# One rotation of three PSUM banks for all transposes and small products, and a changed order of the opening, in a cluster attention followed by two feed-forward layers

## The chip, the cores and the metric

The kernel runs on one core of a Trainium2 chip. The metric is the device time of one execution in microseconds (us), the median of several runs. Engines are named as in the profile: PE is TensorE (PEld its weight loads), DVE is VectorE, ACT is ScalarE, POOL is GpSimd, SP is SyncE, which issues the DMAs here.

## What is computed

```python
q_assign = np.argmax(np.einsum('bhsd,hcd->bhsc', q_n, c_n), axis=-1)
k_assign = np.argmax(np.einsum('bhsd,hcd->bhsc', k_n, c_n), axis=-1)
mask = q_assign[:, :, :, None] == k_assign[:, :, None, :]
scores = np.where(mask, scale * np.matmul(q, k.transpose(0, 1, 3, 2)), -1000000000.0)
attn = np.exp(scores - np.max(scores, axis=-1, keepdims=True))
attn = attn / (np.sum(attn, axis=-1, keepdims=True) + 1e-09)
x = np.matmul(attn, v)                          # 2 x 8 heads, 768 x 64, 16 clusters a head
h = x @ w_in;  x = (np.maximum(h, 0) + alpha * np.minimum(h, 0)) @ w_out      # 1536 x 512 x 2048
h = x @ w2_in; x = (np.maximum(h, 0) + np.log1p(np.exp(-np.abs(h)))) @ w2_out
```

Queries, keys and centroids are normalized first (`q_n`, `k_n`, `c_n`). All of it is float32; the kernel splits each operand into a high part that TensorE takes at full rate and a low rest, and adds three products.

## The kernel before

**Attention** works on 8 pairs of heads. A pair has 12 units, numbered from 0 (so pair 1 starts at unit 12): 2 heads, 3 groups of 256 queries, 2 tiles of 128 queries. The loop over units `u` puts out, in this order: on PE the scores of unit `u` (tile `s`, L721 and L722, four matmuls into a pool of two buffers); on ACT the exponential of unit `u-1` (tile `e`, L736); on DVE the negated row maximum of unit `u` (`nm`, L727); then the steps set down for an early place in `u`; then on PE the six transposes of `e` of unit `u-2`, three to a PSUM bank (`pt`, L749), which ACT copies out as a high part (`ph`, L765) and DVE as the rest (`pl`, L769); then on PE six products with the values (`o`, L779); then the steps set down for a late place in `u`.

**The preparation of a pair** is cut into named steps. For pair `n` they are: `sq`, `fold`, `inv` (squares of the token tile `tok`, their sums on POOL, inverse norms `rinv` through ACT, DVE and POOL, L133 to L142); `hik`, `hiq`, `lok`, `lq` (high and low parts of the transposed tile `dim`, `lq` on DVE, L510); `dk`, `dq` (products with the cluster centroids, tile `dps`, L525, three matmuls each for keys and queries, 0 and 1 for the two halves of the sequence); `de` (ACT copies `dps` to `dsb`, L533); `dt` (six small transposes of `dsb`, L550); `dn`, `mx`, `eq`, `m2` (the arg max, on DVE and POOL, L564 to L604); `ot` (three transposes of the one-hot rows, L614); `mr` (ACT makes mask rows `mrow`, L622); `mk` (SP copies these by DMA into the operands `mq` and `mk` of the scores, L671, L672); `va` (values split on POOL, L686, L687). After a pair, `finish` spreads the sums by three transposes to a bank (`rp_`, L863) and DVE divides (L872).

**What sets the order.** All engines run in the order in which the program puts out instructions (`tc.manual_schedule`). The tables STEADY, FIRST, SECOND, THIRD and LAST give each step a unit, counted from 24 units ahead of its pair: `dk0=4` is the late place of unit 4 of the pair two ahead, `de0=5.5` the early place of unit 6. Pair 1 uses SECOND, pair 2 THIRD, pairs 3 to 6 STEADY. What comes ahead of unit 0 stands in the list PRELUDE (name and pair). `warm` puts out transposes of the identity whose results nobody reads (L334).

**PSUM** has eight banks: `ps_t` two (the `pt` tiles, and a few of pair 0), `ps_o` one, `ps_m` one (all small tiles: `dps`, `dt`, `ot`, `rp_`, and the fourth output chunk of the feed-forward layers), `ps_s` two of two banks each for the scores. A new tile waits until the last reader of the tile that had its bank is done.

**The feed-forward layers** follow: matmuls of 128 x 512 into four banks (`ps_h`, which take over the banks of the scores), and output products in four chunks `c` (accumulators `acc`, L287 and L1310): chunks 0 and 1 in `ps_t`, 2 in `ps_o`, 3 in `ps_m`. Their weights come as 64-bit words and are converted on ACT, DVE and POOL beside the matmuls.

Of the kernel before, what the change touches and what calls it, by code (L numbers as in the profile page):

```python
# [24 lines left out]
    sq0=0, hik0=1, hik1=2, lok=2, hiq0=3, hiq1=3, sq1=3, lt=3.5, fold0=4, lq0=4, dk0=4, dq0=5, de0=5.5,  # L25
    lq1=6.5, dk1=6, dq1=7, de1=7.5, fold1=8, fold2=9, dt=10, ld=10, inv0=11, inv1=11.5, inv2=12, dn=12.5,
# [7 lines left out]
    dl0=12, dl1=12, inv0=12, de0=12.5, de1=12.5, inv1=12.5, inv2=13, dt=13, dn=13.5, op0a=13.5, mx=14,  # L34
    op0b=14.5, op0c=15.5, eq=16, op1a=17.5, m2=18, op1b=18, op1c=18.5, ot0=20, mr0=20.5, ot1=21, mr1=21.5,
    mk0=21.5, va0=22, mk1=22.5, va1=24, lv=25, go=23,
)
THIRD = dict(STEADY, hik0=3, sq0=3, hik1=3, hiq0=4, lok=4, hiq1=5, sq1=5, lt=5.5, lq0=5, dk0=5, fold0=7)
# [22 lines left out]
def kernel(  # L61
# [139 lines left out]
    ps_t = ctx.enter_context(tc.tile_pool(name="ps_t", bufs=2, space=PSUM, reuse_waits="tile"))  # L201
    ps_o = ctx.enter_context(tc.tile_pool(name="ps_o", bufs=1, space=PSUM, reuse_waits="tile"))
    ps_m = ctx.enter_context(tc.tile_pool(name="ps_m", bufs=1, space=PSUM, reuse_waits="tile"))
# [70 lines left out]
    def second(k):  # L274
        layer, g, f = mlp_steps[k]
        gh, gl = acts.pop(k)
        h_, l_ = weights[layer, f][2:4]
        opens, closes = (layer, f) in starts, (layer, f) in ends
        if opens:
            for c in range(4):  # L280
                pool, tag = ((ps_t, "t"), (ps_t, "t"), (ps_o, "o"), (ps_m, "m"))[c]
                accs[c] = pool.tile([P, 512], F32, tag=tag, name=f"acc{c}")
        for c in range(4):
            cs = slice(c * P, (c + 1) * P)
            prods = ((h_[:, cs], gh), (h_[:, cs], gl), (l_[:, cs], gh))
            for n, (a_, b_) in enumerate(prods):
                nc.tensor.matmul(  # L287
                    accs[c], lhsT=a_, rhs=b_, start=opens and n == 0, stop=closes and n == 2
                )
# [28 lines left out]
    with ExitStack() as actx:  # L318
# [40 lines left out]
        def load_tok(n):  # L359
            if n < len(pairs):  # L360
                if n == 1:
                    toks[n] = ap2.tile([P, J, 2, P], F32, tag="ph", name="tok", bufs=2)
                else:
                    toks[n] = ap1.tile([P, J, 2, P], F32, tag="tok", name="tok")
                nc.sync.dma_start(out=toks[n], in_=qk_tok[pairs[n]])
# [26 lines left out]
        cps = ps_m.tile([P, 512], F32, tag="m", name="cps")  # L392
# [35 lines left out]
        def steps_of(n):  # L428
# [87 lines left out]
            def dots(t, prods):  # L516
                if prods[0] == (1, 0):
                    if early and t == 0:
                        q["dps", t] = ps_o.tile([P, 512], F32, tag="o", name="dps")
                    else:  # L520
                        q["dps", t] = ps_m.tile([P, 512], F32, tag="m", name="dps")
# [22 lines left out]
            def _():  # L544
                if first_:
                    dt = ps_t.tile([P, 512], F32, tag="t", name="dt")
                else:
                    dt = ps_m.tile([P, 512], F32, tag="m", name="dt")
# [59 lines left out]
            def onehot(t):  # L608
                if first_:
                    q["ot", t] = ps_t.tile([P, 512], F32R, tag="t", name="ot")  # L610
                else:
                    q["ot", t] = ps_m.tile([P, 512], F32R, tag="m", name="ot")
# [207 lines left out]
        def finish(n):  # L820
# [34 lines left out]
            for t in range(2):  # L855

                def spread(t):
                    if last and t == 1:
                        rp_ = ps_t.tile([P, 512], F32, tag="t", name="rp_")
                    else:  # L860
                        rp_ = ps_m.tile([P, 512], F32, tag="m", name="rp_")
# [66 lines left out]
        at(1)(lambda: warm(8))  # L928
# [363 lines left out]
    def out_product(q, g, c, tick):  # L1292
# [4 lines left out]
        def run():  # L1297
            pool, tag = ((ps_t, "t"), (ps_t, "t"), (ps_o, "o"), (ps_m, "m"))[c]
# [44 lines left out]
    def last_product():  # L1343
# [4 lines left out]
        for n, (pool, tag) in enumerate(((ps_m, "m"), (ps_t, "t"))):  # L1348
# [289 lines left out]
```

## Time and profile before

| | |
|---|---|
| Median of 3 runs | 781.36 us (781.09 to 781.46) |
| The profiled execution | 782.5 us, its span 780.7 us |
| PE, DVE, ACT, POOL busy | 760.1, 650.6, 552.2, 507.9 us |
| Mean granted clock of PE | 0.996 |

The span runs from the first to the last instruction; the execution's own time is 1.8 us longer. Busy time of PE counts a matmul from its start to its modelled end, and matmuls overlap, so it says little by itself: where PE is close to its limit, the distance from one start to the next tells more. The attention ends near 266 us; the rest is the two layers.

### The profile page before, as it was taken

To read this page: it belongs to the slowest core of one execution; us is meant where nothing else is said; L and a number is where in the kernel's file an instruction comes from. 1 tells how busy PE (TensorE), PEld (TensorE's weight loads), DVE (VectorE), ACT (ScalarE), POOL (GpSimd) and SP (SyncE) were. 2 spreads that over 40 slices of the span, in tenths; PEclk is the share of its full clock that TensorE was granted. 3 is DMA by queue.
4 is the path that set the end of the run, shared out by engine and by line. 5 is a ranking of instruction groups with operands and counts; after the bars stand their busy time and mean duration, and the time that the engine had idled before them with its cause. 6 is when DMAs were issued, how large, how long until landed. Compare 5 with 4: busy or idle time off the path is not lost.

```text
span 780.7 us, 12017 instructions
## 1 busy us (share of the span) xinstructions
PE 760.1 (97%) x4073; PEld 651.5 (83%) x4073; DVE 650.6 (83%) x1015; ACT 552.2 (71%) x1130; POOL 507.9 (65%) x510
## 2 busy tenths in 40 slices
PE   7699999999999899999999999999999999999998
PEld 6598999999999788788888888887888888888887
DVE  6778889889899767489967768799989898998965
ACT  5788999999899878365766766856965555655530
POOL 5666677886643545478758778598785766756810
PEclk9999999999999999999999999999999999999999
DMA  9857467566452350012112121211220302212004
GB/s 248 217 147 194 126 179 183 143 158 163 101 132 81 106 182 34 0 55 82 37 72 81 55 81 60 76 54 33 103 80 29 108 27 81 82 54 82 1 0 162
DMA packets 27101, 75.92 MB, mean 97 GB/s; under 512 B 4480, under 2 KB 7680, under 8 KB 27040
## 3 DMA queue, kind: packets, MB, share of 16 engines
q1 hardware_dynamic: 27040, 75.16, 32.9%
q8 instruction: 32, 0.52, 0.3%
q14 instruction: 29, 0.24, 0.1%
HBM read 49.36 MB, written 3.15 MB: 67 GB/s over the span
## 4 chain that ended last, share of the span: by engine, by line
PE 81%; ACT 6%; POOL 4%; DVE 3%; issue 3%; DMA 2%; SPq 0%; POOLq 0%; ACTq 0%; DVEq 0%
PE acc L1310 26%; PE hp L1146 9%; PE x L1146 8%; PE pt L749 7%; PE o L779 7%; PE v L1146 4%; PE acc L287 4%; PE s L721 4%; PE s L722 4%; PE hp L235 3%; PE z L1146 2%; DMA tok<-in_qk_tok_dram 1%; PE dps L525 1%; POOL sq L470 1%; ACT e L736 1%
## 5 line engine op out<-in xcount | busy, mean ns | idle before, releaser
L727 DVE TENSOR_REDUCE nm<-s 128x1 f32<-128x768 f32 x96 | 91.1, 949 | 17.4 <-PE s L722 17.2
L769 DVE TENSOR_TENSOR pl<-pt,ph 128x384 fp32r<-128x384 f32 x192 | 97.6, 550 | 8.3 <-ACT ph L765 7.6
L765 ACT CAST ph<-pt 128x384 fp32r<-128x384 f32 x192 | 84.1, 488 | 15.4 <-PE pt L749 14.7
L736 ACT ACTIVATE e<-s,nm 128x768 f32<-128x768 f32 x96 | 88.2, 918 | 3.4 <-DVE nm L727 2.9
L749 PE MATMUL pt<-ident,e 128*128 128x128 f32 x576 | 83.6, 278 | 6.0 <-DVE pl L769 6.0
L749 PEld LDWEIGHTS pt<-ident,e 128*128 128x128 f32 x576 | 67.4, 142 | 18.5 <-DVE pl L769 15.0
L1326 DVE TENSOR_TENSOR y<-y,acc 128x512 f32<-128x512 f32 x97 | 65.9, 680 | 15.9 <-PE acc L1310 15.6
L1333 POOL TENSOR_TENSOR y<-y,n 128x512 f32<-128x512 f32 x42 | 57.0, 1362 | 32.2 <-ACT n L1323 32.2
L1310 PE MATMUL acc<-oh,gl 128*128 128x512 f32 x190 | 74.0, 389 | 0.0
L1310 PE MATMUL acc<-oh,gh 128*128 128x512 f32 x190 | 74.0, 389 | 0.0
L1310 PE MATMUL acc<-ol,gh 128*128 128x512 f32 x190 | 74.0, 389 | 0.0
L175 DVE SCALAR_TENSOR_TENSOR r<-raw,r 128x512 uint32<-128x512 uint32 x64 | 65.6, 1025 | 4.0 <-issue 3.1
L721 PE MATMUL s<-ak,aq 128*128 128x384 f32 x192 | 68.9, 359 | 0.0
L722 PE MATMUL s<-mk,mq 80*128 80x384 f32 x192 | 65.7, 342 | 2.5 <-DVE mk L633 2.5
L182 POOL TENSOR_TENSOR tw<-m,r 128x512 uint32<-128x512 uint32 x26 | 34.0, 1308 | 48.4 <-DVE r L175 47.4
L187 POOL TENSOR_TENSOR il<-tw,ih 128x512 fp32r<-128x512 f32 x26 | 34.3, 1320 | 34.0 <-ACT ih L186 34.0
L182 POOL TENSOR_TENSOR t<-m,r 128x512 uint32<-128x512 uint32 x38 | 50.1, 1318 | 9.1 <-DVE r L175 9.1
L187 POOL TENSOR_TENSOR ol<-t,oh 128x512 fp32r<-128x512 f32 x32 | 46.8, 1461 | 11.6 <-ACT oh L186 11.6
L170 DVE TENSOR_SCALAR m<-m 128x512 f32<-128x512 f32 x64 | 47.5, 742 | 3.9 <-ACT m L166 3.8
L1146 PE MATMUL hp<-xl,ih 128*128 128x512 f32 x120 | 46.9, 391 | 1.4 <-DVE xl L1365 1.4
L1310 PE MATMUL acc<-gl,oh 128*128 128x512 f32 x120 | 46.8, 390 | 0.0
L1146 PE MATMUL hp<-xh,il 128*128 128x512 f32 x120 | 46.7, 390 | 0.0
(295 smaller groups left out, 2357.7 us busy)
## 6 DMA issues: line engine op xcount, KB each, us to landing
raw<-in_w_in_dram SPq DMA_DIRECT2D x32, 512.0 KB, 3.2
raw<-in_w_out_dram SPq DMA_DIRECT2D x32, 512.0 KB, 3.3
tok<-in_qk_tok_dram SPq DMA_DIRECT2D x8, 768.0 KB, 6.0
ak<-hi SPq DMA_DIRECT2D x31, 192.0 KB, 3.0
dim<-in_qk_dim_dram SPq DMA_DIRECT2D x6, 768.0 KB, 5.7
aq<-hi SPq DMA_DIRECT2D x16, 192.0 KB, 3.6
aq<-lo SPq DMA_DIRECT2D x16, 192.0 KB, 4.0
rawv<-in_v_dram SPq DMA_DIRECT2D x8, 384.0 KB, 4.0
```

What stands on the lines that cost most here:

```text
L182: nc.gpsimd.tensor_tensor(out=t.bitcast(U32), in0=mu, in1=r, op=ALU.add)
L187: nc.gpsimd.tensor_tensor(out=low, in0=t, in1=high.bitcast(F32), op=ALU.subtract)
L721: nc.tensor.matmul(s[:, c, 0:HS], lhsT=aq[:, qs], rhs=ak[:, ks], start=True, stop=False)
L722: nc.tensor.matmul(s[:, c, 0:HS], lhsT=mq[:, qs], rhs=mk[:, ks], start=False, stop=True)
L727: nc.vector.tensor_reduce(out=nm, in_=st[u]["s"][:, :, 0:HS], axis=AX.XY, op=ALU.max, negate=True)
L736: nc.scalar.activation(out=e.rearrange("p (a j) c -> p a (j c)", a=2), in_=st[u]["s"][:, :, 0:HS], func=AF.Exp, bias=st[u]["nm"], scale=1. ...
L749: nc.tensor.transpose(pt[:, j * P : (j + 1) * P], st[u]["e"][:, 3 * a + j, :], ident)
L765: nc.scalar.copy(out=dh, in_=src)
L769: nc.vector.tensor_tensor(out=dl, in0=src, in1=dh.bitcast(F32), op=ALU.subtract)
L1146: nc.tensor.matmul(o, lhsT=x_, rhs=y_, start=start and j == 0 and n == 0, stop=stop and j == len(ah) - 1 and n == 2, skip_group_check=chain,)
L1310: nc.tensor.matmul(acc, lhsT=a_, rhs=b_, start=s_ == 0 and n == 0, stop=s_ == 1 and n == 2)
L1326: nc.vector.tensor_tensor(out=y, in0=y, in1=acc, op=ALU.add)
```

## The change

All tiles of `ps_m` go into `ps_t`, which gets three banks; the pool `ps_m` is gone. Steps get other places: in STEADY `dk0` goes from unit 4 to 5 (where `dq0` is), `lq1` from the early place of unit 7 to the late place of unit 6, `dk1` from 6 to 7 (where `dq1` is), `dt` from 10 to 12. In THIRD (pair 2) `dk0` and `dq0` go to 6, `lq1` and `de0` to 7, `dk1` and `dq1` to 8. In SECOND (pair 1) `inv2` and `dt` go half a unit later, `eq` one unit earlier, `va1` half a unit later. In PRELUDE `lq0 1` and `lq1 1` go behind the mask rows of pair 0. The token tile of pair 0 is loaded by two DMAs, and the eight `warm` transposes of unit 1 are left out.

```diff
-    sq0=0, hik0=1, hik1=2, lok=2, hiq0=3, hiq1=3, sq1=3, lt=3.5, fold0=4, lq0=4, dk0=4, dq0=5, de0=5.5,
-    lq1=6.5, dk1=6, dq1=7, de1=7.5, fold1=8, fold2=9, dt=10, ld=10, inv0=11, inv1=11.5, inv2=12, dn=12.5,
+    sq0=0, hik0=1, hik1=2, lok=2, hiq0=3, hiq1=3, sq1=3, lt=3.5, fold0=4, lq0=4, dk0=5, dq0=5, de0=5.5,
+    lq1=6, dk1=7, dq1=7, de1=7.5, fold1=8, fold2=9, dt=12, ld=10, inv0=11, inv1=11.5, inv2=12, dn=12.5,
...
 SECOND = dict(
-    dl0=12, dl1=12, inv0=12, de0=12.5, de1=12.5, inv1=12.5, inv2=13, dt=13, dn=13.5, op0a=13.5, mx=14,
-    op0b=14.5, op0c=15.5, eq=16, op1a=17.5, m2=18, op1b=18, op1c=18.5, ot0=20, mr0=20.5, ot1=21, mr1=21.5,
-    mk0=21.5, va0=22, mk1=22.5, va1=24, lv=25, go=23,
+    dl0=12, dl1=12, inv0=12, de0=12.5, de1=12.5, inv1=12.5, inv2=13.5, dt=13.5, dn=13.5, op0a=13.5, mx=14,
+    op0b=14.5, op0c=15.5, eq=15, op1a=17.5, m2=18, op1b=18, op1c=18.5, ot0=20, mr0=20.5, ot1=21, mr1=21.5,
+    mk0=21.5, va0=22, mk1=22.5, va1=24.5, lv=25.5, go=23,
 )
-THIRD = dict(STEADY, hik0=3, sq0=3, hik1=3, hiq0=4, lok=4, hiq1=5, sq1=5, lt=5.5, lq0=5, dk0=5, fold0=7)
+THIRD = dict(STEADY, hik0=3, sq0=3, hik1=3, hiq0=4, lok=4, hiq1=5, sq1=5, lt=5.5, lq0=5, dk0=6, dq0=6, de0=6.5, lq1=7, dk1=8, dq1=8, de1=8.5, fold0=7)
...
-    "dh1 1", "op1a 0", "op1b 0", "op1c 0", "minus_alpha", "dn 0", "mx 0", "eq 0", "m2 0", "lq0 1",
-    "lq1 1", "ot0 0", "ot1 0", "rq0 0", "rk1 0", "rk0 0", "rq1 0", "go 0", "mr0 0", "mr1 0", "mk1 0", "ld 1",
+    "dh1 1", "op1a 0", "op1b 0", "op1c 0", "minus_alpha", "dn 0", "mx 0", "eq 0", "m2 0",
+    "ot0 0", "ot1 0", "rq0 0", "rk1 0", "rk0 0", "rq1 0", "lq0 1", "lq1 1", "go 0", "mr0 0", "mr1 0", "mk1 0", "ld 1",
...
-    ps_t = ctx.enter_context(tc.tile_pool(name="ps_t", bufs=2, space=PSUM, reuse_waits="tile"))
+    ps_t = ctx.enter_context(tc.tile_pool(name="ps_t", bufs=3, space=PSUM, reuse_waits="tile"))
     ps_o = ctx.enter_context(tc.tile_pool(name="ps_o", bufs=1, space=PSUM, reuse_waits="tile"))
-    ps_m = ctx.enter_context(tc.tile_pool(name="ps_m", bufs=1, space=PSUM, reuse_waits="tile"))
...
-                pool, tag = ((ps_t, "t"), (ps_t, "t"), (ps_o, "o"), (ps_m, "m"))[c]
+                pool, tag = ((ps_t, "t"), (ps_t, "t"), (ps_o, "o"), (ps_t, "t"))[c]
...
-                nc.sync.dma_start(out=toks[n], in_=qk_tok[pairs[n]])
+                for cut in (slice(0, 3), slice(3, J)) if n == 0 else (slice(0, J),):
+                    nc.sync.dma_start(out=toks[n][:, cut], in_=qk_tok[pairs[n]][:, cut])
...
-                        q["dps", t] = ps_m.tile([P, 512], F32, tag="m", name="dps")
+                        q["dps", t] = ps_t.tile([P, 512], F32, tag="t", name="dps")
...
-                    q["ot", t] = ps_m.tile([P, 512], F32R, tag="m", name="ot")
+                    q["ot", t] = ps_t.tile([P, 512], F32R, tag="t", name="ot")
...
-        at(1)(lambda: warm(8))
```

The other lines of the diff put `cps`, `dt`, `rp_` and the accumulators of chunk 3 from `ps_m` into `ps_t` in the same way.

**PE in the opening**, units 1 and 2 (`s` scores, `wps` the warm transposes, `pt` transposes of the probabilities of unit 0, `dt` small transposes of pair 1). Before:

```order
L550 MATMUL dt<-ident,dsb 128x64 x6
L334 MATMUL wps<-ident 128x128 x8
L721 MATMUL s<-ak,aq 128x384
L722 MATMUL s<-mk,mq 128x384
L721 MATMUL s<-ak,aq 128x384
L722 MATMUL s<-mk,mq 128x384
L749 MATMUL pt<-ident,e 128x128 x6
```

With the change:

```order
L721 MATMUL s<-ak,aq 128x384
L722 MATMUL s<-mk,mq 128x384
L721 MATMUL s<-ak,aq 128x384
L722 MATMUL s<-mk,mq 128x384
L550 MATMUL dt<-ident,dsb 128x64 x6
L749 MATMUL pt<-ident,e 128x128 x6
```

The scores of unit 2 stand ahead of the small transposes, which are followed by the transposes of the probabilities at once.

**POOL at the end of pair 0**, unit 12 (`s_810` and `s_792` the norms of pair 2 in work, `vv` values of pair 1, `sq` squares of pair 3). Before:

```order
L139 TENSOR_TENSOR s_810<-s_810,s_793 128x24
L686 CAST vv<-rawv 128x6x64
L687 TENSOR_TENSOR vv<-rawv,vv 128x6x64
L141 TENSOR_SCALAR s_810<-s_810 128x24
L453 TENSOR_TENSOR sq<-tok 128x768
```

With the change:

```order
L139 TENSOR_TENSOR s_792<-s_792,s_775 128x24
L141 TENSOR_SCALAR s_792<-s_792 128x24
L453 TENSOR_TENSOR sq<-tok 128x768
L686 CAST vv<-rawv 128x6x64
L687 TENSOR_TENSOR vv<-rawv,vv 128x6x64
```

The two instructions of the values have gone behind the norms.

**PE at a pair's end**, from unit 9 of pair 2 on. Before:

```order
L614 MATMUL ot<-identr,oh 64x128 x3
L721 MATMUL s<-ak,aq 128x384
L722 MATMUL s<-mk,mq 128x384
L721 MATMUL s<-ak,aq 128x384
L722 MATMUL s<-mk,mq 128x384
L749 MATMUL pt<-ident,e 128x128 x6
L779 MATMUL o<-ph,vv 128x256 x6
L550 MATMUL dt<-ident,dsb 128x64 x6
```

With the change, two units later (unit 0 of pair 3):

```order
L721 MATMUL s<-ak,aq 128x384
L722 MATMUL s<-mk,mq 128x384
L749 MATMUL pt<-ident,e 128x128 x6
L779 MATMUL o<-ph,vv 128x256 x6
L550 MATMUL dt<-ident,dsb 128x64 x6
L721 MATMUL s<-ak,aq 128x384
```

The small transposes `dt` have left unit 10 and stand between units 0 and 1 of the next pair.

## Rows read from the trace of the kernel before

**Rows 1.** Windows by stage: us; busy PE, PEld, DVE, ACT, POOL; clock; DMA share.

```profile
0.00:22.80 22.80, 16.54 (x95) 14.73 (x95) 15.31 (x30) 13.75 (x28) 13.64 (x45) 0.93 0.89 236
22.80:53.20 30.40, 25.85 (x189) 22.76 (x189) 24.29 (x38) 23.65 (x56) 18.91 (x24) 1.00 0.76 189
53.20:85.40 32.20, 30.63 (x219) 28.46 (x218) 26.74 (x47) 27.18 (x66) 22.08 (x29) 0.95 0.59 153
85.40:231.70 146.30, 146.29 (x1095) 136.14 (x1093) 133.86 (x239) 137.20 (x335) 103.19 (x131) 1.00 0.62 152
231.70:266.60 34.90, 31.45 (x231) 28.30 (x230) 31.30 (x59) 33.20 (x78) 13.63 (x16) 1.00 0.31 103
266.60:780.70 514.10, 509.32 (x2257) 421.09 (x2256) 419.11 (x607) 317.19 (x572) 336.42 (x267) 1.00 0.19 66
```

**Rows 2.** Chain of waits in the opening: start us, us, what.

```profile
4.08 11.19 DMA tok<-in_qk_tok_dram
...
22.19 0.34 ACT s L133
...
22.78 0.97 ACT e L736 x2
...
25.12 1.02 PE wps L334 x8
```

**Rows 3.** Timeline of ACT, then PE, in the opening; idle before in brackets.

```profile
8.71 1.58 ACT L451 ACTIVATE sq<-tok 128x768 f32<-128x768 f32 x2 [2.15 <-DMA tok<-in_qk_tok_dram]
...
20.97 0.41 PE L722 MATMUL s<-mk,mq 80*128 80x384 f32 x1 [2.52 <-DVE mk L633]
...
37.85 0.39 PE L525 MATMUL dps<-lo,chz 128*64 128x384 f32 x1 [1.94 <-DMA rest<-tmp]
...
53.16 0.34 PE L721 MATMUL s<-ak,aq 128*128 128x384 f32 x1
...
59.83 1.01 PE L749 MATMUL pt<-ident,e 128*128 128x128 f32 x6 [1.57 <-DVE pl L769]
```

**Rows 4.** Timeline of DVE, then POOL, then DVE in the opening.

```profile
33.41 2.12 DVE L587 SCALAR_TENSOR_TENSOR dn<-dn,rank 128x384 f32<-128x384 f32 x1
...
56.40 1.01 POOL L687 TENSOR_TENSOR vv<-rawv,vv 128x384 fp32r<-128x384 f32 x1
57.49 0.21 POOL L141 TENSOR_SCALAR s<-s 128x24 f32<-128x24 f32 x1
...
57.74 0.30 DVE L142 RECIPROCAL rinv<-s 128x24 f32<-128x24 f32 x1 [1.50 <-POOL s L141]
```

**Rows 5.** Chain of waits in pair 3, from its unit 0 to the next pair.

```profile
115.97 0.66 PE pt L749 x6
...
117.33 0.33 PE s L721
...
118.19 1.00 PE pt L749 x6
...
120.61 0.99 PE pt L749 x6
...
142.19 0.52 PE dt L550 x6
...
145.16 0.18 PE s L722
```

**Rows 6.** SP's issue of the mask rows of pair 4, and its landing time.

```profile
142.41 0.58 SPq L672 DMA_DIRECT2D mk<-mrow  x1
...
mk<-mrow SPq DMA_DIRECT2D x1, 48.0 KB, 2.1
```

**Rows 7.** Windows: the granted clock (third number from the end) around two falls.

```profile
13.10:16.50 3.40, 3.40 (x18) 3.29 (x17) 3.12 (x7) 3.24 (x7) 1.82 (x1) 0.50 1.02 213
16.50:24.00 7.50, 4.11 (x26) 3.12 (x24) 6.08 (x7) 4.70 (x10) 6.49 (x9) 1.00 0.81 165
...
60.90:64.30 3.40, 3.40 (x17) 3.30 (x15) 2.55 (x4) 2.09 (x5) 3.24 (x4) 0.50 0.82 178
```

More of the change, by code (lines that the diff above doesn't have):

```diff
@@ L391 @@
         warm(18, ps_s)
-        cps = ps_m.tile([P, 512], F32, tag="m", name="cps")
+        cps = ps_t.tile([P, 512], F32, tag="t", name="cps")
         nc.tensor.transpose(cps[:, 0:P], cnrm, ident)
@@ L547, in _ @@
                 else:
-                    dt = ps_m.tile([P, 512], F32, tag="m", name="dt")
+                    dt = ps_t.tile([P, 512], F32, tag="t", name="dt")
                 for j in range(J):
@@ L860, in spread @@
                     else:
-                        rp_ = ps_m.tile([P, 512], F32, tag="m", name="rp_")
+                        rp_ = ps_t.tile([P, 512], F32, tag="t", name="rp_")
                     for j in range(3):
@@ L1297, in run @@
         def run():
-            pool, tag = ((ps_t, "t"), (ps_t, "t"), (ps_o, "o"), (ps_m, "m"))[c]
+            pool, tag = ((ps_t, "t"), (ps_t, "t"), (ps_o, "o"), (ps_t, "t"))[c]
             acc = pool.tile([P, 512], F32, tag=tag, name=f"acc{c}")
@@ L1347, in last_product @@
         t0 = g * G + c * P
-        for n, (pool, tag) in enumerate(((ps_m, "m"), (ps_t, "t"))):
+        for n, (pool, tag) in enumerate(((ps_t, "t"), (ps_t, "t"))):
             cut = slice(n * HB, (n + 1) * HB)
```

## Prediction

> **What bounds the kernel now.** I read four views in this order: busy time by stage, the chain of waits, the timelines where the chain leaves PE, and the landing of the DMAs that PE reads.
>
> The stages [rows 1] show where time can be had at all. From 266.6 us on PE is busy 509.3 of 514.1 us, so the layers are bound by matmuls that the change leaves alone. In the middle of the attention, 85.4 to 231.7 us, PE is called busy all the time (146.29 of 146.30), ACT has 137.2 and DVE 133.9: PE is the bound with the others close behind, and a stall there can only be seen in stretched starts. The opening is slack: from 22.8 to 53.2 us PE has 25.9 of 30.4 us, from 53.2 to 85.4 us 30.6 of 32.2, part of that at a lower clock. The last pair, 231.7 to 266.6 us, is ACT's (33.2 of 34.9).
>
> In the opening the chain [rows 2] comes from the DMA of pair 1's token tile (4.08 us, 11.19 long), through its squares and sums, to an ACT logarithm at 22.19 us; only behind this, in ACT's order, stands the first exponential, at 22.78 us. After that PE itself is on the chain with 1.02 us of warm transposes. Two idle times of PE follow [rows 3]: 1.94 us ahead of a cluster product at 37.85 us and 1.57 us ahead of transposes at 59.83 us. The profile blames a DMA for the first, which nothing on PE reads; the product at 37.85 us reads the low part of the queries, which DVE makes behind an `eq` that took 2.12 us [rows 4]. The second comes from DVE, idle 1.50 us because POOL did the values of pair 1 (1.01 us for the second of two instructions) ahead of a 0.21 us norm step at 57.49 us [rows 4].
>
> In a steady pair the chain stays on PE, and its pieces say where PE is stretched [rows 5]: six transposes cost 0.66 us where nothing is late, and 1.00 and 0.99 us in units 1 and 2, where they wait for DVE's reading of the bank; the first score of unit 1 takes 0.33 us where a score takes 0.18.
>
> **The change, part by part.** The sum is made against the profiled execution of 782.5 us (span 780.7), which lies 1.1 us over the median of 781.36; the differences hold for both.
>
> *Up to the first exponential: 0.* The split token load lets ACT begin its squares of pair 0 before 8.71 us, of the 2.15 us it waits there perhaps half, and moving `lq0 1`, `lq1 1` lets the first scores start before 20.97 us [rows 3], where DVE was doing those two ahead of the mask rows. Both lie beside the chain from pair 1's token tile, which is not touched: the DMA share up to 22.8 us is 0.89 [rows 1], so one more issue moves no byte earlier or later. If the cover went, the gain were up to 1 us. Bounds: a loss of 0.5 us (one issue more on SP ahead of that load) and a gain of 0.6 us.
>
> *Warm transposes out, scores of unit 2 ahead of `dt`: 1.7 us.* ACT frees the score bank at 22.78 + 0.97 = 23.75 us, while PE sits until 24.6 us (25.12 less the 0.52 us of `dt` [rows 5]) for `dsb`. The four scores (4 x 0.18 = 0.72 us) now run in that hole, and the 1.02 us of warm transposes are gone: the first probabilities are transposed at about 25.1 us, where the warm ones began, and not at 25.12 + 1.02 + 0.72 = 26.86 us. Late next is the maximum of unit 2, which moves up with its scores, so ACT follows. Bounds 1.0 (the warm ones alone) and 1.74.
>
> *`eq` of pair 1 a unit earlier, products of pair 2 a unit later: 1.9 us, less 0.7.* The idle 1.94 us goes: `dq0` stands one unit behind `lq0`, and DVE no longer has `eq` between. Against it, in unit 8 both `ot0` of pair 1 and `dk1` of pair 2 now take a bank: with the two `pt` tiles that is four tiles in a unit for three banks, so `dk1` waits for DVE to read a `pt` of its own unit, which DVE does behind that unit's maximum. No row shows this wait; the nearest are the 0.34 us by which transposes wait for DVE in rows 5 and the 1.57 us of rows 3, and I take 0.7 us, nearer the first, as it is a wait for the same reading. Bounds of the two together: 0 and 1.9, since DVE could be late by something else.
>
> *Values of pair 1 behind the norms: 2.9 us.* The 1.50 us that DVE waited, 1.57 us on PE, go. The same idle time stands ahead of a stretch of 3.4 us in which the granted clock was 0.50 [rows 7], that is 1.2 GHz; at 2.4 GHz the PE work in it is 1.7 us. Without the idle time I expect no fall there, but DVE and ACT were not idle for all of it, so I take 1.3 of the 1.7. Bounds 1.6 and 3.3. POOL's squares of pair 3 (ahead of the values now) delay nothing that is read before the second head of pair 1, six units on.
>
> *Third bank and moved `dt` in the steady pairs: 0.5 us a pair, 2.5 us.* The stretch in units 1 and 2 is 0.34 + 0.33 us, and the score's is 0.15: 0.82 us a pair [rows 5]. With `dt` (0.52 us) between units 0 and 1, DVE and ACT catch up there; unit 2 comes behind a unit without a small tile, so its first `pt` has a bank of its own. `dt` itself only moves: pair 0 loses one, pair 6 gains one. But it was cover: the mask rows, issued at 142.41 us, land 2.1 us later, 144.5 us [rows 6], and PE reads them in the score at 145.16 us [rows 5], 0.65 us on. PE now comes there 0.52 us sooner, or 0.7 with the slower score behind `dt`: the spare is used up, and I take 0.2 us of waiting. `dk` and `dq` in one unit leave DVE and ACT without scores for half a microsecond longer there, for 0.1 us more. 0.82 - 0.2 - 0.1 = 0.5, times the five pairs 2 to 6. Bounds 0 and 0.82 a pair, 0 and 4.1 together.
>
> *Last pair and layers: 0.* The last pair is ACT's, whose order is kept. In the layers chunk 3 joins the rotation, but it was every third tile of chunks 0, 1 and 3 and three banks come round in three: each accumulator falls on the bank that it waits for today. Bounds: a loss of 0.5 and a gain of 1.0. The layers start when the attention is done, so what is won ahead of them comes out at the end.
>
> Sum: 1.7 + 1.9 - 0.7 + 2.9 + 2.5 = 8.3 us, 774.2 us for the profiled execution, 773.0 us for the median.
>
> **A rule against it.** After an idle time of 1.57 us the clock fell to 0.50; behind one of 2.52 us at 18.5 to 21.0 us [rows 3] it stayed at 1.00 from 16.5 to 24 us, though PE was busy only 4.1 of 7.5 us [rows 7]. So the rows leave the fall open, and the sum holds nothing for taking the warm transposes out. The Trainium skill (TensorE: Matmul & The Clock Gate, What's actually happening) says that "the default state is throttled, and activity releases the throttle"; by that rule, taking activity out of a stretch that is already thin asks for one more fall, which would make the sum 6.6 us and not 8.3. The 1.0 at 16.5 to 24 us speaks against it, the two falls for it.
>
> **Rivals.**
> 1. *The clock falls in the opening.* The scores of units 0 to 2 spread over 17 to 24 us with holes, the warm transposes are gone, and a stretch like that of 60.9 us comes where PE is on the path: 3.4 us at half rate are 1.7 us lost. 781.4 - 8.3 + 1.7 = 774.8 us. Chance 0.14. This is the rule above as a mechanism of this kernel.
> 2. *The DMAs pace the opening.* The share is 0.89 up to 22.8 us and 0.76 up to 53.2 us [rows 1], and the tiles of pair 2 and the mask rows stand in one queue. Then PE runs ahead only to wait for them, `eq` and the values bring nothing, and 1.7 + 2.5 us stay: 777.2 us. For it: the chain starts with such a load. Against: both idle times come from DVE, not from a landing. Chance 0.12.
> 3. *The rotation ties PE to ACT's readers, and the kernel is slower.* A pair has seven small tiles (two `dps`, one `dt`, two `ot`, two `rp_`). Each now takes a turn, and a `pt` two or three tiles on waits until ACT or DVE has read it. ACT is busy 137.2 of 146.3 us and reads four of the seven behind an exponential. Where such a read ends late, the transposes stretch as in rows 5, by 0.34 us. With n of seven late in six pairs that is 2.0n us against 5.8 won in the opening: from three on it loses, and with five it is 781.4 + 10.2 - 5.8 = 785.8 us. Against it: the read comes early in the next unit, and the `pt` that wants its bank stands half a unit behind it. Chance 0.07.
> 4. *The attention ends sooner and the layers wait.* The conversion of the first weights starts 14 units ahead of the end, by loads and ACT work; if these do not move up, the first products wait: about 781 us. Against it: they are put out by units, and the DMA share is 0.31 there [rows 1]. Chance 0.05.
>
> **How the numbers follow.** The forecast has 0.62 and takes 768 to 777 us by its bounds: the upper ends give 0.6 + 1.74 + 1.9 + 3.3 + 4.1 + 1.0 = 12.6 us, 768.7 us; 777 us is where the steady pairs give nothing and the values only 1.6 us (1.7 + 1.2 + 1.6 = 4.5). Rivals 1 and 2 are inside. Low 767.5 us leaves a little for a shorter wait than I see; high 779 us has all terms but the warm transposes at their lower ends (1.0 + 1.6 - 0.5 = 2.1 us). Outside lie rivals 3 and 4 and some of the forecast's own tails, not over 0.2. A measurement of this kernel tells 0.2%, 1.6 us, from no change. Faster: the forecast and rivals 1 and 2, 0.88; the same: rival 4, 0.05; slower: rival 3, 0.07.
>
> **What would show it.** Right: the first exponential still near 22.8 us; transposes of unit 0 near 25.1 us; no idle time of more than 0.3 us ahead of a cluster product in units 5 to 7, some 0.7 us in unit 8; unit 12 at about 50 us for 53.16 [rows 3]; no DVE wait on POOL's norm step; the clock at 1.00 from 25 us on; about 143.8 us for the five pairs that take 146.3 now [rows 1]; transposes at 0.66 us in units 1 and 2, and a score at the pair's start that waits up to 0.3 us for mask rows. Wrong: transposes stretched behind small tiles (rival 3), a first exponential that moved by over 0.5 us, a clock of 0.50 after 20 us, or a stage behind 266 us that changed its length by over 0.5 us.

## The result, and the profile after

| | before | with the change |
|---|---|---|
| Median of the runs, side by side | 781.23 us (780.39 to 781.46) | 773.75 us (773.39 to 775.15) |
| Ratio, 95% interval | | 0.9911 (0.9896 to 0.9926) |
| The profiled execution, its span | 782.5, 780.7 us | 773.39, 771.6 us |

The kernel is 7.5 us faster; 773.0 us was forecast. The stages of the profile after, cut at the same events as [rows 1] (first exponential, unit 12, unit 24, unit 84, first product of the layers; units are counted through, so unit 12 is the first of pair 1), in the same columns:

```profile
0.00:21.60 21.60, 16.49 (x95) 14.15 (x95) 14.50 (x31) 13.71 (x28) 13.58 (x45) 0.92 0.89 252
21.60:47.00 25.40, 23.64 (x173) 21.52 (x173) 21.86 (x38) 23.32 (x57) 18.22 (x23) 1.00 0.84 217
47.00:76.10 29.10, 29.00 (x219) 27.25 (x217) 26.39 (x47) 26.32 (x67) 22.12 (x30) 1.00 0.66 170
76.10:221.30 145.20, 143.77 (x1101) 137.25 (x1099) 134.12 (x239) 136.59 (x336) 103.66 (x132) 1.00 0.64 155
221.30:257.10 35.80, 32.39 (x231) 29.73 (x230) 32.11 (x60) 33.94 (x79) 14.07 (x16) 0.96 0.31 101
257.10:771.60 514.50, 509.55 (x2257) 421.15 (x2256) 418.70 (x605) 316.88 (x571) 335.98 (x267) 1.00 0.20 66
```

Against [rows 1], stage by stage: 1.2 us won up to the first exponential (0 was forecast), 5.0 in the rest of pair 0 (1.7 + 1.9 - 0.7 = 2.9), 3.1 in pair 1 (2.9), 1.1 in pairs 2 to 6 (2.5), and 0.9 and 0.4 lost in the last two (0 each). The sum is 9.1 us of span between two single executions, where the medians are 7.5 us apart; the forecast was 8.3. That the sum came out so near is in part luck: against the forecast the terms that were off differ by +1.2, +2.1, -1.4 and -1.3 us. The experiments are about those.

The timeline of PE in the opening (start, us, engine, line, operation, count, idle before):

```profile
22.56 0.44 PE L721 MATMUL s<-ak,aq 128*128 128x384 f32 x1 [1.31 <-ACT e L736]
...
23.97 0.87 PE L749 MATMUL pt<-ident,e 128*128 128x128 f32 x6
...
39.44 0.39 PE L525 MATMUL dps<-hi,chz 128*64 128x384 f32 x1 [0.29 <-DVE pl L769]
...
46.99 0.34 PE L721 MATMUL s<-ak,aq 128*128 128x384 f32 x1
47.43 0.42 PE L722 MATMUL s<-mk,mq 80*128 80x384 f32 x1
```

Unit 12 starts at 46.99 us for 53.16 [rows 3]. The second score of unit 12 stands 0.44 us behind the first, where two scores follow at 0.18: that is the wait for mask rows. The two idle times of rows 3 are gone; the one idle time ahead of a cluster product stands in unit 8, behind DVE's reading of a `pt`, as forecast, but it is 0.29 us long. What the rows of PE's waits say of pair 0 (engine, line, waited for: us in total, times, longest), before from 24.5 to 53.2 us:

```profile
PE dps L525 <- DMA rest<-tmp: 1.9, 1, 1.9
PE dt L550 <- ACT dsb L533: 1.4, 1, 1.4
PE pt L749 <- DVE pl L769: 1.2, 2, 0.6
```

and after, from 22 to 47 us:

```profile
PE s L721 <- ACT e L736: 1.3, 1, 1.3
PE pt L749 <- DVE pl L769: 0.5, 1, 0.5
PE dps L525 <- DVE pl L769: 0.3, 1, 0.3
```

The third row of before is a wait for DVE to read a tile out of one of the two banks; 0.7 us of it went, and the prediction had not counted it. The steady pair, in the chain of waits of pair 3 (start us, us, what), answers to [rows 5]:

```profile
106.28 0.42 PE s L722
...
107.05 0.66 PE pt L749 x6
...
108.42 0.52 PE dt L550 x6
108.94 0.38 PE s L721
...
109.85 0.66 PE pt L749 x6
...
111.93 0.66 PE pt L749 x6
```

Transposes take 0.66 us in units 0, 1 and 2; the 1.00 and 0.99 us are gone. But the score that reads the mask rows, in unit 0, took 0.18 us [rows 5] and takes 0.42 now, with 0.18 us of nothing ahead of it. SP's issue of these rows:

```profile
104.06 0.58 SPq L672 DMA_DIRECT2D mk<-mrow  x1
```

It landed 2.13 us later, at 106.19 us, and the score starts 0.09 us behind that. Last, the clock (third number from the end): one fall ahead of the first exponential, none at unit 14, and a new one in the last pair.

```profile
11.90:15.30 3.40, 3.40 (x18) 3.25 (x18) 3.09 (x8) 3.40 (x7) 1.72 (x1) 0.50 1.04 244
15.30:24.00 8.70, 6.08 (x39) 4.43 (x37) 6.05 (x10) 5.93 (x13) 7.56 (x14) 1.00 0.78 171
24.00:76.00 52.00, 51.10 (x379) 47.55 (x379) 46.85 (x82) 47.14 (x117) 38.25 (x47) 1.00 0.76 196
...
254.20:257.60 3.40, 3.40 (x17) 3.13 (x17) 2.64 (x7) 2.47 (x6) 3.25 (x3) 0.51 0.00 0
```

### The profile page after: what moved, and what is told of

Same layout as the page of the kernel before. It is cut to its first block, busy times and chain, and to the rows that moved or that the text cites. A ratio compares the mean times of both kernels' runs of the same rounds, so it can differ in the third digit from the quotient of the medians.

```text
span 771.6 us, 12011 instructions
## 1 busy us (share of the span) xinstructions
PE 754.8 (98%) x4065; PEld 651.1 (84%) x4065; DVE 647.7 (84%) x1015; ACT 550.8 (71%) x1130; POOL 507.6 (66%) x510
## 4 chain that ended last, share of the span: by engine, by line
PE 83%; ACT 7%; DVE 4%; DMA 2%; POOL 2%; issue 2%; SPq 0%; DVEq 0%; ACTq 0%; POOLq 0%
PE acc L1309 26%; PE hp L1145 9%; PE x L1145 8%; PE o L779 8%; PE pt L749 7%; PE v L1145 4%; PE s L722 4%; PE acc L286 4%; PE s L721 4%; PE hp L234 4%; PE z L1145 2%; PE dps L525 2%; ACT e L736 1%; DMA raw<-in_w_in_dram 1%; ACT ph L765 1%
## 5 line engine op out<-in xcount | busy, mean ns | idle before, releaser
L749 PE MATMUL pt<-ident,e 128*128 128x128 f32 x576 | 81.3, 275 | 2.8 <-DVE pl L769 2.8
L779 PE MATMUL o<-ph,vv 128*128 128x256 f32 x288 | 46.0, 295 | 0.8 <-DVE xs L804 0.6
```

The source lines that it names most:

```text
L749: nc.tensor.transpose(pt[:, j * P : (j + 1) * P], st[u]["e"][:, 3 * a + j, :], ident)
L779: nc.tensor.matmul(acc[key][:, 0:QG], lhsT=vv[:, j, 2 * hh : 2 * hh + 2, :].rearrange("p a d -> p (a d)"), rhs=grp[key][part][:, j, :], st ...
```

## The experiments

Each ran beside the kernel before on one chip. "Ratio" is to that kernel, with its 95% interval, of some 0.0017 to each side (1.3 us); differences below about 1.5 us between two of these kernels are therefore read from the profiles, one execution each, and called so. e1 to e4, e5 to e8 and e9 to e12 each shared a chip and the runs of before (medians 781.59, 781.52 and 781.71 us).

### Order without banks, banks without order

e1 is the new order with `ps_t` of two banks and `ps_m` of one, as before; e2 is the old order with the three banks of the change.

```diff
-    ps_t = ctx.enter_context(tc.tile_pool(name="ps_t", bufs=3, space=PSUM, reuse_waits="tile"))
+    ps_t = ctx.enter_context(tc.tile_pool(name="ps_t", bufs=2, space=PSUM, reuse_waits="tile"))
+    ps_m = ctx.enter_context(tc.tile_pool(name="ps_m", bufs=1, space=PSUM, reuse_waits="tile"))
```

> The changed order of instructions with the banks as they were (two for the transposes, one for all small tiles). If the third bank in the rotation carries what the prediction put on the steady pairs, the 0.82 us a pair of stretched transposes and scores come back: pairs 2 to 6 take 146 to 148 us in place of 145.2, the whole 776 to 778 us, and the score of unit 12 still starts at 47 to 48 us, since the opening was won by the order. If the order alone does it (rival: the bank is not what the transposes wait for), the whole stays within 0.5 us of 773.8 and the pairs at 145.2. If products of one unit in one bank make each other wait, unit 12 itself comes over 1.5 us later and the whole passes 779 us.

> The rotation of three banks with the old order and tables, the old single load and the warm transposes. If the rotation is worth what stands for the steady pairs alone, pairs 2 to 6 take 143 to 145 us (0.3 to 0.8 us a pair under 146.3), the opening stays (unit 12 near 53 us), and the whole is 777.5 to 779.5 us. If the rotation helps only together with the moved steps (a small tile in units 4, 6 and 10 takes the bank that a transpose needs), the pairs stay at 146.3 or grow and the whole is 780.5 to 783 us. With e1, the two give the part of the order, of the banks and of both together.

Measured: e1 777.09 us, ratio 0.9941 (0.9923 to 0.9959); e2 781.49 us, 0.9994 (0.9983 to 1.0005). The pairs 2 to 6, by stage, first in e1, then in e2:

```profile
78.30:224.80 146.50, 146.37 (x1101) 136.17 (x1099) 133.93 (x239) 137.71 (x335) 103.69 (x132) 1.00 0.63 153
```

```profile
83.30:228.70 145.40, 145.40 (x1095) 136.33 (x1093) 133.89 (x239) 137.47 (x335) 103.06 (x131) 1.00 0.62 154
```

So 146.5 and 145.4 us, for 146.3 before and 145.2 with both: in the steady pairs the order alone wins nothing, the banks alone 0.9 us, and the banks carry what is won there. In the opening it is the other way: unit 24 comes at 78.3 us in e1, at 83.3 in e2, for 85.4 and 76.1. The wins of 7.0 and 2.1 us are nearly the 9.3 of both, but all three are measured against the one profile that has the fall of the clock at 60.9 us [rows 7], which is some 1.4 us of each (an estimate, from units 14 and 15 of e2 below). Where e1 loses most in the opening is unit 8, in PE's timeline:

```profile
40.97 0.39 PE L526 MATMUL dps<-hi,chz 128*64 128x384 f32 x1 [1.34 <-ACT mrow L623]
```

With one bank for small tiles, the moved products wait for ACT to read the one-hot transposes of the same unit: 1.34 us, where the rotation of three leaves 0.29. The new order needs the banks for its full gain; 4.5 us come without them.

e2's median missed the 777.5 to 779.5 us expected of it. Its profiled execution was 778.75 us, the lowest of its twelve, at a granted clock of 0.996; six of the others have 0.989 and 781.45 to 784.1 us. What the rotation alone is worth in the whole therefore stays open, between nothing (the medians) and 3.7 us (the spans of the two profiled executions, 777.0 and 780.7 us). Of these 3.7 us, 1.5 lie in the layers, where e2 lacks a wait that most profiles have (last section), and some 1.4 are the fall that it lacks.

### The first exponential: one load again

```diff
-                for cut in (slice(0, 3), slice(3, J)) if n == 0 else (slice(0, J),):
+                for cut in (slice(0, J),):
```

> The changed kernel with the token tile of pair 0 loaded by one DMA again. The first exponential came 1.15 us earlier (21.63 for 22.78 us), which the prediction had at 0; pair 1's token tile landed at 13.68 us for 15.28. If the split did this, the tile lands near 15.3 us again, the first exponential starts at 22.5 to 22.9 us and the whole is 774.6 to 775.0 us. If it comes from the two low parts of pair 1 that moved behind the mask rows, or from the DMAs varying from run to run, the first exponential stays near 21.6 us and the whole within 0.3 us of 773.8.

Measured: 773.79 us, 0.9902 (0.9887 to 0.9918), first exponential at 21.58 us. The split moves neither. What moved the first exponential shows when e2, with the old order, is laid beside it. Its token tile landed at 13.46 us (15.28 in the profile of before), and ACT squared it without a wait; yet its first exponential came at 22.44 us. DVE, then ACT, of e2:

```profile
15.91 3.31 DVE L509 SCALAR_TENSOR_TENSOR lo<-dim,hi 128x384 fp32r<-128x384 f32 x2
19.25 1.26 DVE L632 TENSOR_SCALAR mk<-ot,mscale,mbias 16x384 fp32r<-16x384 f32 x2
21.45 0.96 DVE L726 TENSOR_REDUCE nm<-s 128x1 f32<-128x768 f32 x1 [0.94 <-PE s L721]
```

```profile
19.96 0.66 ACT L628 ACTIVATE mq<-ot,mbias,mscale 16x384 fp32r<-16x384 f32 x1 [2.15 <-DVE mk L632]
20.63 1.23 ACT L621 ACTIVATE mrow<-ot,mbias,mscale 64x384 fp32r<-64x384 f32 x2
...
22.44 0.90 ACT L735 ACTIVATE e<-s,nm 128x768 f32<-128x768 f32 x1
```

The two low parts of pair 1 hold up the mask rows on DVE, these hold up ACT (2.15 us), and the logarithm stands behind ACT's mask rows. The first scores wait for the same rows, so their row maximum `nm` ends at 22.41 us, 0.03 us ahead of the exponential. In the changed order DVE makes the mask rows first, and the chain of waits goes through the token tile and POOL's sums instead; with that tile at 14.70 us in e4 the first exponential is at 21.99 us. e2 and e3 both load the tile at once and differ up to this point in the place of the two low parts. So two paths of nearly one length ended at the first exponential of [rows 2]: in the profile of before ACT's mask rows and POOL's sums both end within 0.03 us of the logarithm's start. The prediction saw one.

### The eight warm transposes, and dt behind the scores

```diff
+        at(1)(lambda: warm(8))
```

> The changed kernel with the eight warm transposes of unit 1 put back. By the prediction they stand on the path with their 1.02 us: the first transposes of probabilities start about 1 us later (25 us for 23.97), and 774.5 to 775.0 us come out at the end. If PE has slack again a little later (ACT or DVE bound units 1 to 12), unit 12 comes at 47.0 to 47.3 us all the same and the whole stays within 0.3 us of 773.8. If they hold the clock up (rival), a fall after 20 us would be missing that the changed kernel has: it has none there, so no gain is expected.

Measured: 773.13 us, 0.9889 (0.9876 to 0.9902). No loss: in PE's timeline

```profile
21.55 1.04 PE L333 MATMUL wps<-ident 128*128 128x128 f32 x8
23.02 0.45 PE L721 MATMUL s<-ak,aq 128*128 128x384 f32 x1 [0.43 <-ACT e L736]
```

the 1.04 us lie in the 1.31 us that the changed kernel waits for the score bank at this point. The expected second half was then tried alone, the small transposes of pair 1 ahead of those scores again:

```diff
-    ... inv2=13.5, dt=13.5, dn=13.5, ...
+    ... inv2=13.5, dt=13, dn=13.5, ...
```

> The changed kernel with the small transposes of pair 1 ahead of the scores of unit 2 again, the eight warm transposes still out. Putting the warm ones back cost nothing (unit 12 at 47.34 us in that run, its first exponential 0.45 us later), so if the prediction's 1.7 us is real, all of it must hang on this: the scores of unit 2 start behind dt, 0.7 to 1.7 us later, the first transposes of probabilities at 25 to 25.7 us for 23.97, unit 12 1 us or more later, and the whole is 774.5 to 775.5 us. If PE has room in units 3 to 6 (rival), unit 12 is within 0.4 us of 47.0 and the whole of 773.8.

Measured: 774.68 us, 0.9910 (0.9894 to 0.9925), the same ratio as the change itself. In its profile the transposes of unit 0 start at 25.13 us (23.97), as expected:

```profile
22.80 0.95 PE L550 MATMUL dt<-ident,dsb 64*128 64x64 f32 x6 [1.67 <-ACT dsb L533]
23.68 0.69 PE L721 MATMUL s<-ak,aq 128*128 128x384 f32 x1
```

but the clock was at 0.50 from some 23 us on in that execution, so how much of the 1.2 us is the order is not settled: between 0 and 1.2 us, and in the whole not to be told from nothing.

### The values, the comparison and the products

e5 puts the values of pair 1 ahead of the norm step again, e6 the comparison a unit later, e12 the products of pair 2 a unit earlier:

```diff
-    ... inv2=13.5, ... va1=24.5, lv=25.5, go=23,
+    ... inv2=13, ... va1=24, lv=25, go=23,
```

```diff
-    op0b=14.5, op0c=15.5, eq=15, op1a=17.5,
+    op0b=14.5, op0c=15.5, eq=16, op1a=17.5,
```

```diff
-THIRD = dict(..., lq0=5, dk0=6, dq0=6, de0=6.5, lq1=7, dk1=8, dq1=8, de1=8.5, fold0=7)
+THIRD = dict(..., lq0=5, dk0=5, fold0=7)
```

> The changed kernel with the values of pair 1 (and the load behind them) ahead of POOL's norm step again. The prediction put 2.9 us on this: DVE waits 1.5 us for POOL at the norm step, PE about as long in units 14 and 15, and the clock falls behind it. If so, units 14 and 15 (2.08 and 2.07 us from start to start in the changed kernel) take 3 us more together and the whole is 776 to 777 us. The rotation alone already took units 14 and 15 from 7.64 to 5.78 us without this edit, which speaks for a smaller part: by that rival the edit is worth 1.0 to 1.7 us, no fall of the clock at units 14 to 16, and the whole is 774.7 to 775.5 us. Nothing (773.8) if POOL is early by now.

> The changed kernel with the comparison of pair 1 a unit later again, behind DVE's low part of the queries of pair 2 in time but not in the table. The prediction put 1.9 us on the comparison and the products of pair 2 together. If the comparison is what made the cluster products wait, a wait of 1 us or more comes back ahead of a cluster product in units 5 to 7 and the whole is 774.8 to 775.7 us. If the products' later place alone did it (rival), units 4 to 8 keep their lengths within 0.3 us and the whole stays within 0.4 us of 773.8.

> The changed kernel with the products of pair 2 a unit earlier again (with the late place of the comparison undone in an earlier run, this is the other half of that term). If the earlier comparison alone removed the wait, the low part of the queries is ready in time: units 4 to 7 keep their lengths, unit 8 loses the wait that the two products and the one-hot transposes make there (3.81 us from start to start in the changed kernel, 3.1 to 3.3 here), unit 12 comes within 0.4 us of 47.0 or earlier, and the whole is 773.2 to 774.0 us. If the products need the later place too, a wait of 0.7 us or more comes ahead of one in unit 5 or 6, and the whole is 774.5 us or more.

Measured: e5 775.13 us, 0.9922 (0.9906 to 0.9939); e6 775.81 us, 0.9931 (0.9911 to 0.9951); e12 775.15 us, 0.9913 (0.9896 to 0.9930).

In e5 DVE waits for POOL at the norm step again, in its timeline:

```profile
52.12 0.30 DVE L142 RECIPROCAL rinv<-s 128x24 f32<-128x24 f32 x1 [1.63 <-POOL s L141]
```

as long as before, but PE loses only 0.56 us of idle behind it, where it lost 1.57 [rows 3]:

```profile
53.84 0.41 PE L749 MATMUL pt<-ident,e 128*128 128x128 f32 x2 [0.56 <-DVE dn L564]
```

No fall of the clock followed. Units 14 and 15 took 1.0 us more together (5.14 for 4.15 us from start to start), the lower end of the rival. Before they took 7.64 us, in e1 (the order without the banks) 4.57, in e2 (the banks without the order) 5.78. So the order alone removes 3.1 of the 3.5 us and the banks alone 1.9: the two overlap, and with the banks in place the move is worth 1.0 us. The 1.9 us of e2 are not all the banks' work: PE still idles 1.10 us there for 1.57, and the rest, some 1.4 us by these rows, is that the clock did not fall. Why it fell in the profile of before alone stays open.

In e6, PE waits 0.87 us in unit 6 for DVE, but at the transposes, not at a product; the products wait for nothing. Its profiled execution also had the clock at 0.50 from 23.6 to 30.4 us, so its unit 12 at 49.9 us is not the comparison's work alone; beside e11, which fell alike, unit 6, behind the fall in both, takes 4.20 us for 3.11. In e12 a product does wait, and not for DVE:

```profile
33.37 0.39 PE L525 MATMUL dps<-lo,chz 128*64 128x384 f32 x1 [1.23 <-POOL lo L505]
```

This is the low part of the keys, which POOL makes. So there are two late operands: the queries' low part, behind the idle 1.94 us of [rows 3], which the earlier comparison brings, and behind it the keys'. Before, the keys' part came just in time (its product started at 35.17 us, where POOL ends at 35.11); with PE some 3 us earlier it is late, unless the products stand a unit later. Units 5 to 8 took 13.3 us before and take 11.3 in the changed kernel; with one move taken back they take 12.0 (e6) and 12.2 us (e12), so each alone brings over half, and both together more. In e12 unit 8 is free of its wait: 2.25 us for 3.81, of which two products are 1.04, which leaves 0.5 for the wait. Unit 12 of e12 is at 48.08 us for 46.99. In the whole e12 has the ratio of the change, so this loss is read from the profiles alone.

### Two covers for the mask rows

```diff
-    lq1=6, dk1=7, dq1=7, de1=7.5, fold1=8, fold2=9, dt=12, ld=10,
+    lq1=6, dk1=7, dq1=7, de1=7.5, fold1=8, fold2=9, dt=11, ld=10,
```

```diff
-    ... ot0=20, va0=20, mr0=20.5, ot1=21, mr1=21.5, mk0=21.5,
+    ... ot0=19, va0=20, mr0=19.5, ot1=20, mr1=20.5, mk0=20.5,
```

> The changed kernel with the small transposes dt of pairs 2 to 7 one unit earlier, ahead of the pair's first score and no more behind it. If they were the cover of the mask rows, the second score of unit 0 takes 0.18 us for 0.42, unit 0 of each pair 0.3 to 0.45 us less from start to start, and six pairs give 1.5 to 2.5 us: 771.3 to 772.3 us. If the bank that dt takes in unit 11 makes the transposes of units 0 and 1 wait (rival), they stretch by 0.3 us a pair and the whole stays within 0.5 us of 773.8, or is up to 1 us longer.

> The changed kernel with the one-hot transposes, the mask rows and the first of their two DMAs one unit earlier in pairs 2 to 7, and dt left where it is. If the mask rows are late, the second score of unit 0 takes 0.18 us for 0.42, each of six pairs wins 0.3 to 0.45 us, and the whole is 771.3 to 772.3 us. If POOL has the one-hot rows only just in time (rival), PE waits for them in unit 7 and the time is 773.8 to 776 us. Three small tiles stand in unit 7 then (two products and the first one-hot transposes): a stretch of 0.3 us in unit 7 or 8 would take the gain back.

Measured: e7 772.24 us, 0.9884 (0.9866 to 0.9902); e8 784.47 us, 1.0049 (1.0030 to 1.0069). The chain of waits of e7 at the pair's start:

```profile
134.97 0.52 PE dt L550 x6
135.49 0.37 PE s L721
135.86 0.18 PE s L722
```

The wait for the mask rows is gone here, and in pairs 1 to 5; pairs 6 and 7 still have it (in pair 6 the rows landed 2.7 us after their issue). Pairs 2 to 6 take 143.5 us for 145.2:

```profile
77.10:220.60 143.50, 143.27 (x1093) 136.40 (x1093) 132.46 (x238) 136.20 (x333) 103.22 (x131) 1.00 0.63 156
```

143.8 us were forecast for the change, with 0.2 us a pair for this wait. Of the 1.7 us, 0.5 is one `dt` that pairs 2 to 6 no longer hold: unit 11 of pair 0 has it now and takes 2.67 us for 2.07. Pairs 3 to 5 win 0.2 us each, less than was expected, since the transposes of unit 3 are stretched, as the rival said, from 0.74 to 0.98 us:

```profile
142.95 0.98 PE pt L749 x6
```

Unit 84 starts 0.65 us earlier than in the changed kernel (220.63 for 221.28 us). The intervals of e7 and of the change overlap, so that e7 is faster is read from these rows and not shown by the times. In e8 the rows come early at a price many times theirs, far above the 773.8 to 776 us of the rival. PE waits for POOL's one-hot rows in unit 7 of each pair; in pair 3:

```profile
PE ot L614 <- POOL oh L604: 1.8, 1, 1.8
```

and behind this wait the clock stood at 0.51 from 131.5 to 134.9 us. Making rows earlier needs the arg max earlier, which this table does not have; moving PE's own work ahead of their reader costs 0.2 us a pair in unit 3.

### The clock, and the best version

```diff
+            if u == NU - 2 and a == 1:
+                fill(10, 2)
...
+                if u == NU:
+                    fill(6, 3)
```

e10 is e7 with the eight warm transposes of e4; e11 is e7 with `fill`, which puts transposes of the identity into banks of the layers.

> The kernel with dt in unit 11 (the one that beat both) and the eight warm transposes of unit 1 put back: 772.0 to 772.5 us if they lie in PE's wait for the score bank as they did in the changed kernel, 773 us and unit 12 at 48.5 us or later if they lie on the path, under 771.7 us only if they keep the clock up somewhere later.

> The kernel with dt in unit 11 and sixteen transposes of the identity in PE's two waits of the last pair (ten ahead of the second half of unit 94's transposes, six behind it). A fall of the clock there costs 0.9 to 1.2 us: from unit 84 to the first product of the layers the profiled runs take 34.9 us without one and 35.6 to 36.2 us with one, and it is in five of nine of them. If activity there keeps the clock up, the stretch takes 34.9 us, no run shows the fall, the mean granted clock of the runs is 0.997 or more and the median 771.2 to 771.9 us. If falls come where they will (rival), the clocks of the runs spread as before (0.991 to 0.998) and the median stays at 772.2 us; if the transposes delay ACT, the stretch takes 35.3 us or more.

Measured: e10 771.71 us, 0.9871 (0.9854 to 0.9888), the lowest median of all, and faster than the change (intervals apart); that it is faster than e7 is not shown. e11 772.75 us, 0.9884 (0.9869 to 0.9898): nothing won, and the clocks of its runs spread from 0.993 to 0.998, as the rival said. Its last pair took 34.9 us from unit 84 to the layers with no fall of the clock, but so it did in e4, e5, e6, e7, e9, e10 and e12; whether the filling does anything stays open. What e11 showed by chance is a fall in the opening. Up to its last pair it runs e7's instructions; the same stretch in e11, then in e7:

```profile
20.70:31.50 10.80, 9.94 (x43) 8.68 (x42) 8.16 (x14) 7.58 (x19) 5.61 (x12) 0.53 0.93 237
```

```profile
20.70:31.50 10.80, 8.99 (x61) 7.34 (x60) 9.38 (x17) 9.73 (x25) 6.32 (x12) 1.00 0.79 232
```

Its unit 12 starts at 50.16 us, that of e7 at 48.07.

## Why the prediction was right, and where it was off

**Up to the first exponential: 0, measured 1.2.** The step that failed is "both lie beside the chain from pair 1's token tile". The split does lie beside it (e3); the two low parts stood on a second path of the same length, through DVE's and ACT's mask rows (e2). The first exponential waited for both, and in the profile of before both ended within 0.1 us of each other, so the chain named one. Part of the 1.2 us may be chance: the token tile landed at 15.28 us there, and at 12.59 to 14.70 us in the thirteen other profiles, with and without the split.

**Warm transposes and scores ahead of `dt`: 1.7.** The transposes of unit 0 start 2.7 us earlier, 1.2 of it from the first exponential, so 1.5 is left. Of the two parts the forecast gave 1.0 to the warm transposes: that is wrong once the scores stand ahead of `dt`, where PE waits for the score bank and has room for them (e4). What the scores ahead of `dt` bring is not settled (e9), so no run shows the 1.7 us as the work of this move.

**Comparison and products: 1.9 less 0.7.** The wait for a bank in unit 8 is there as forecast, at 0.5 us for 0.7 (0.4 to 0.8 in the other profiles of this order and these banks). The gain is larger: units 5 to 8 take 2.0 us less for the forecast's 1.2 net. The reason was half right. The queries' low part behind `eq` is one late operand; POOL's low part of the keys, which the forecast does not name, is the next as soon as the first is in time (e12). Each move alone brings 1.1 to 1.3 of the 2.0 us (e12, e6).

**Not in the forecast:** 0.7 us in units 3 and 4 (0.5 with the banks alone, 0.3 with the order alone), and 0.8 in units 9 to 11, which lose `dt` to pair 1 (booked in the forecast under the steady pairs).

**Values behind the norms: 2.9, measured 3.1 for pair 1.** Right in size; the cause is in part open. The wait for POOL is real, and the order without the banks wins 2.6 us in pair 1 (e1). But with the banks the move is worth 1.0 us (e5), not 1.57: the banks alone cut PE's idle time there to 1.10 us (e2). The 1.3 us for the clock is not shown to belong to the idle time: PE idles there in e2 (1.10 us) and e5 (0.56 us), and neither has a fall behind it, nor has any other profile but that of before.

**Steady pairs: 2.5, measured 1.1.** Of the 0.82 us of stretch a pair, the 0.67 of the transposes went; the 0.15 of the score did not, as the first score of unit 1 takes 0.38 us behind `dt`. The main step that failed is "I take 0.2 us of waiting" for the mask rows. It is 0.4 us in pairs 3 to 5, 0.75 in pair 2 and 0.55 in pair 6, together 2.6 us for the 1.0 reckoned. The spare was read too large: the chain [rows 5] sets the score at 145.16 us, but the timeline of before starts it at 145.00, 0.5 us behind the landing and not 0.65:

```profile
145.00 0.34 PE L722 MATMUL s<-mk,mq 80*128 80x384 f32 x1
```

The pair count failed as well: pairs 3 to 5 win 0.36 us each, pair 2 with its longer wait 0.06, and pair 6, which has little stretch to win but takes a `dt`, nothing. The price of 0.1 us for two products in one unit was not there.

**Last pair and layers: 0, measured a loss of 1.3.** The last pair took 35.8 us for 34.9, with the clock at 0.51 for 3.4 us. From unit 84 to the layers all profiles without a fall there have 34.9 to 35.0 us, and the five with one (the change, e1, e2, e3, e8) 35.2 to 36.2; so the 0.9 goes with the clock. The layers' 0.3 to 0.4 us go with it too: their first twelve products, the first of them still at the lower clock, take 3.06 us for 2.77, and PE waits for nothing there. The forecast held no fall in the last pair.

**The rivals.** Rival 3 has hardly a sign: the transposes of unit 3, behind a small tile, take 0.74 us for 0.66 (0.98 in e7). Rival 2 (777.2 us) is out by the time; rival 4 too, as the layers start without a wait. Rival 1, the clock, is real but not constant: of twelve profiles with the new order three (e6, e9, e11) have a fall that begins after 20 us and lasts 6.8 to 10.2 us, and e5 has one from 18.2 to 21.6 us in place of the earlier one. The price is 2.1 us at unit 12 (e11 against e7). The rival's 1.7 us was near this by luck, since it reckoned with 3.4 us on PE's path. The Trainium skill (TensorE: Matmul & The Clock Gate, What's actually happening), which the prediction weighed against the change, says that activity releases the throttle; the profiles with the eight transposes back (e4, e10) have no such fall, but neither have seven without them, so the rows do not decide it.

**The bounds.** In the range, the upper end of 779 us leaves out one of the two losses of 0.5 us that the terms allow (with both it is 779.8 us); this changes nothing here.

## What to carry to other kernels

Sharing banks between two users pays where one of them has bursts: three banks in turn cut PE's wait in unit 8 from 1.34 to 0.29 us, and in the steady pairs the moved order won only with them. A small step of an engine's own that stands ahead of a late operand is cover: it hides the wait. Find what it hides before moving it (`dt` is 0.5 us long, and without it the mask rows cost 0.4 us or more a pair). Where a chain names one wait, look for a second path that ends within half a microsecond of it. Look for late operands one by one: when the first comes in time, the next is the one that is waited for (e12). And before a term is booked for a fall of the clock, look whether a second execution has that fall.

## What the runs showed of the hardware that was not expected

The clock's falls differ between executions of instructions that are the same: up to the last pair, e7 falls from 12.3 to 15.7 us and e11 from 20.8 to 31.0. Eleven of the fourteen profiles have a fall between 10 and 17 us, where the kernels hardly differ; e4 has none in the whole attention:

```profile
12.00:16.00 4.00, 3.84 (x28) 3.05 (x28) 3.65 (x9) 4.00 (x8) 1.85 (x1) 1.00 1.05 224
```

In some kernels the time follows the mean granted clock: e3 took 773.06 to 773.79 us at 0.996, 775.13 at 0.993, 776.37 at 0.989. In others it does not: e6's fastest run, 774.02 us, is at 0.993 and its slowest, 778.36, at 0.996. A single execution can be 2 or 3 us off its kernel's median, and the clock alone does not tell by how much.

In the layers, two waits of PE for DVE between 526 and 541 us, 1.4 us together, are there in all profiles but two (e2, e11), whose layers are 1.1 to 2.1 us shorter than all others. In the changed kernel, DVE, then POOL:

```profile
522.27 1.54 DVE L170 TENSOR_SCALAR m<-m 128x512 f32<-128x512 f32 x1
```

```profile
520.86 2.67 POOL L1454 TENSOR_TENSOR y<-y 128x512 f32<-128x512 f32 x2
```

and in e2:

```profile
529.51 0.41 DVE L170 TENSOR_SCALAR m<-m 128x512 f32<-128x512 f32 x1
```

```profile
528.10 2.98 POOL L1454 TENSOR_TENSOR y<-y 128x512 f32<-128x512 f32 x2
```

The same instruction takes 0.41 or 1.54 us. The long one ends 0.28 us behind POOL's second addition. In e2, where the short one comes at the change from the first addition to the second, POOL's two take 0.31 us longer. PE then does not wait for DVE, and the layers take 512.7 us for 514.5. The Trainium skill (SBUF — State Buffer, SBUF: two separate sides) says that GpSimd and DVE, the latter in a mode that uses both ports or with two inputs from SBUF, share one pair of ports as an exclusive lock, held for a whole instruction. The rows fit this; that this `TENSOR_SCALAR` runs in such a mode no row shows.
